# A SwiGLU block: x chunk 0 in two transposing DMAs, eight depth-0 matmuls first, weights in need order over two issuing engines

## The chip, the cores and the metric

One core of one Trainium2 chip. The time is that of one execution on the device, in microseconds (us), without a profile; runs differ by a few tenths of a microsecond, so a difference of less than one per cent needs several rounds on the same chip. A profile is one further look at the same program; its span is about 1.8 us shorter than the time of the same execution.

## The reference

```python
B, S, D, F = 1, 2048, 512, 1376          # bf16 inputs
def reference(x, w_gate, w_up, w_down):
    g = silu(x @ w_gate)
    u = x @ w_up
    return (g * u) @ w_down
```

## The kernel before

Tokens are cut into four chunks of 512, D into four depths of 128, F into ten tiles of 128 and a rest of 96. x is transposed by the DMA on its way in, so that a depth lies on the partitions. For each chunk and tile, TensorE (PE) runs four matmuls for gate and four for up (one per depth, 128x512 each), ScalarE (ACT) applies silu, VectorE (DVE) multiplies. Then 16 token groups are multiplied with w_down. All loads are issued by SyncE (SP), weights in slabs of tiles with all depths:

```python
N_WARM = 11
slabs = [(0, 1), (1, 2), (2, 4), (4, 7), (7, NFT)]
...
def xT_dma(eng, c):
    return eng.dma_start_transpose(
        xT_sb[:, :, c * SC:(c + 1) * SC], xf[c * SC:(c + 1) * SC, :]).then_inc(s_xT[c], 16)

@block.sync
def _(sp):
    xT_dma(sp, 0)
    for si in range(len(slabs)):
        wg_slab_dma(sp, si)
        wu_slab_dma(sp, si)
    ...                                        # rest of up, x chunks 1 to 3, w_down, stores

@block.tensor
def _(pe):
    for i in range(N_WARM):                    # warm-up matmuls on constants
        pe.matmul(banks[7][:, :], lhsT=ones_w, rhs=ones_m, start=True, stop=True)
    for c in range(NSC):
        pe.wait_ge(s_xT[c], 16)
        for ft in range(NFF):
            ...                                # wait for the gate slab and a free bank
            for dk in range(KD): ...           # four gate matmuls into psG[n % 3]
            ...                                # wait for the up slab and a free bank
            for dk in range(KD): ...           # four up matmuls into psU[n % 2]

@block.scalar
def _(act):
    act.activation(adummy[:, 0:4], zero_c, ACT.Silu)   # loads the table early
    ...
```

## Time and profile before

The median was 122.76 us in three runs.

The page of the kernel before: busy time and its share of the span by engine, then the chain that ended last, by engine.

```profile
PE 117.9 (97%) x550; PEld 53.3 (44%) x550; DVE 43.8 (36%) x64; ACT 30.2 (25%) x51; POOL 0.2 (0%) x4
...
PE 97%; DVE 0%; issue 0%
```

PE is the bottleneck. Its head, in the timeline of PE alone (start, duration, engine, line, what, how many, and in brackets how long PE was idle before and what ended that):

```profile
0.77 4.85 PE L167 MATMUL bank<-const-bfloat16-1.0 128*128 128x512 bf16 x11 [0.77 <-PEq L322]
5.54 1.42 PE L179 MATMUL bank<-xT_sb,w_sb 128*128 128x512 bf16 x4
6.79 1.03 PE L191 MATMUL bank<-xT_sb,w_sb 128*128 128x512 bf16 x4
7.66 1.03 PE L179 MATMUL bank<-xT_sb,w_sb 128*128 128x512 bf16 x4
```

The first real matmul starts at 5.54 us. From 6.58 us on they start 0.216 us apart; the warm-up matmuls and the first three real ones start 0.38 to 0.43 us apart, that is at about half speed. The granted clock in the records is 1.00 in all this time, so half speed is read from the starts.

The loads at the head as SP issues them (start and duration of the issue):

```profile
0.74 1.40 SPq L128 DMA_TRANSPOSE xT_sb<-in_x_dram  x1
2.20 0.66 SPq L116 DMA_DIRECT2D w_sb<-in_w_gate_dram  x1
2.92 0.48 SPq L123 DMA_DIRECT2D w_sb<-in_w_up_dram  x1
```

By the trace's semaphore updates, x lands at 4.92 us and the first gate slab (128 KB) at 5.41. The first real matmul needs both; the warm-up matmuls fill the time until then (the last starts at 4.99), so PE is hardly idle.

### The profile page before, as it was taken

What the parts mean: (1) busy time and instruction counts of PE and PEld (TensorE: products, weight loads), DVE (VectorE), ACT (ScalarE), POOL (GpSimd) and SP (SyncE); (2) the same over time, 40 slices, a digit from 0 to 9 for tenths busy, and PEclk for the clock granted to TensorE, in tenths of its full rate; (3) what the DMA queues carried; (4) which work ended last, traced back from release to release, by engine and by line L of the source; (5) the groups of instructions that cost most, each with busy time, mean ns of one, the idle gap of its engine ahead of it and who ended that gap; (6) DMA issues with size and microseconds to landing.
All of it is one profiled execution on the core that took longest, in us unless ns stands there. A gap on an engine that the chain in (4) does not pass through costs nothing.

```text
span 121.1 us, 1391 instructions
## 1 busy us (share of the span) xinstructions
PE 117.9 (97%) x550; PEld 53.3 (44%) x550; DVE 43.8 (36%) x64; ACT 30.2 (25%) x51; POOL 0.2 (0%) x4
## 2 busy tenths in 40 slices
PE   7999999999999999999999999999999999999991
PEld 2244444444444444444444444444444444444470
DVE  0024334444334444334444334467242233224221
ACT  4032333262333272333262333230000000000010
POOL 0000000000000000000000000000000000000000
PEclk9999999999999999999999999999999999999999
DMA  3999999900000000000000000000211211121121
GB/s 67 255 283 372 262 241 225 369 20 0 0 0 0 0 0 5 0 0 3 3 0 0 0 0 0 5 0 0 87 43 43 87 43 49 49 81 43 43 74 56
DMA packets 17990, 8.51 MB, mean 70 GB/s; under 512 B 11360, under 2 KB 17984, under 8 KB 17984
## 3 DMA queue, kind: packets, MB, share of 16 engines
q1 hardware_dynamic: 17984, 8.42, 25.6%
q8 instruction: 4, 0.07, 0.2%
q14 instruction: 2, 0.02, 0.0%
HBM read 4.23 MB, written 2.10 MB: 52 GB/s over the span
## 4 chain that ended last, share of the span: by engine, by line
PE 97%; DVE 0%; issue 0%
PE bank L245 32%; PE bank L179 29%; PE bank L191 29%; PE bank L167 4%; PE bank L204 3%; PE bank L215 2%; DVE o_sb L308 0%; PE bank L220 0%
## 5 line engine op out<-in xcount | busy, mean ns | idle before, releaser
L284 DVE TENSOR_TENSOR hT_sb<-sg_sb,bank 128x512 bf16<-128x512 f32 x40 | 27.5, 688 | 44.9 <-PE bank L191 44.8
L179 PE MATMUL bank<-xT_sb,w_sb 128*128 128x512 bf16 x160 | 41.5, 382 | 0.0
L191 PE MATMUL bank<-xT_sb,w_sb 128*128 128x512 bf16 x160 | 41.1, 379 | 0.0
L245 PE MATMUL bank<-wd_sb,hT_sb 128*128 128x512 bf16 (+3 forms) x187 | 38.3, 367 | 0.0
L261 ACT ACTIVATE sg_sb<-bank 128x512 f32<-128x512 f32 x40 | 23.8, 596 | 44.7 <-PE bank L179 44.7
L245 PEld LDWEIGHTS bank<-wd_sb,hT_sb 128*128 128x128 bf16 (+1 forms) x187 | 18.1, 97 | 20.3 <-issue 0.4
L179 PEld LDWEIGHTS bank<-xT_sb,w_sb 128*128 128x128 bf16 x160 | 15.6, 98 | 19.8 <-DMA xT_sb<-in_x_dram 0.8
L191 PEld LDWEIGHTS bank<-xT_sb,w_sb 128*128 128x128 bf16 x160 | 15.6, 98 | 18.9
L308 DVE CAST o_sb<-bank 128x512 bf16<-128x512 f32 (+1 forms) x16 | 10.8, 675 | 24.9 <-PE bank L245 24.9
L275 ACT ACTIVATE o_sb<-bank 128x256 bf16<-128x256 f32 x1 | 0.4, 383 | 37.6 <-PE bank L245 37.6
L167 PE MATMUL bank<-const-bfloat16-1.0 128*128 128x512 bf16 x11 | 4.9, 628 | 0.8 <-PEq L322 0.8
L289 DVE TENSOR_TENSOR hT_sb<-sgx_sb,bank 32x512 bf16<-32x512 f32 x4 | 2.8, 692 | 5.3 <-ACT sgy_sb L266 5.3
L204 PE MATMUL bank<-xT_sb,w_sb 128*128 128x512 bf16 x16 | 4.1, 379 | 0.0
L265 ACT ACTIVATE sgx_sb<-bank 32x512 f32<-32x512 f32 x4 | 2.4, 588 | 4.5 <-PE bank L204 4.5
L167 PEld LDWEIGHTS bank<-const-bfloat16-1.0 128*128 128x128 bf16 x11 | 1.5, 140 | 3.3 <-issue 3.3
L296 DVE TENSOR_TENSOR hT_sb<-sgy_sb,bank 64x512 bf16<-64x512 f32 x4 | 2.7, 684 | 0.1
L204 PEld LDWEIGHTS bank<-xT_sb,w_sb 128*128 128x128 bf16 x16 | 1.6, 98 | 1.9
L266 ACT ACTIVATE sgy_sb<-bank 64x512 f32<-64x512 f32 x4 | 2.4, 589 | 0.0
L215 PE MATMUL bank<-xT_sb,w_sb 128*64 128x512 bf16 x8 | 1.9, 382 | 0.0
L220 PE MATMUL bank<-xT_sb,w_sb 128*64 128x512 bf16 x8 | 1.9, 382 | 0.0
L254 ACT ACT_TABLE_LOAD x1 | 1.3, 1283 | 0.7 <-PEq L322 0.7
L215 PEld LDWEIGHTS bank<-xT_sb,w_sb 128*64 128x64 bf16 x8 | 0.8, 110 | 1.0 <-issue 0.4
(6 smaller groups left out, 1.4 us busy)
## 6 DMA issues: line engine op xcount, KB each, us to landing
out_dram<-o_sb SPq DMA_DIRECT2D x15, 128.0 KB, 1.7
wd_sb<-in_w_down_dram SPq DMA_DIRECT2D x1, 1280.0 KB, 6.3
w_sb<-in_w_gate_dram SPq DMA_DIRECT2D x1, 480.0 KB, 6.2
w_sb<-in_w_up_dram SPq DMA_DIRECT2D x1, 448.0 KB, 6.8
w_sb<-in_w_gate_dram SPq DMA_DIRECT2D x1, 384.0 KB, 4.8
w_sb<-in_w_up_dram SPq DMA_DIRECT2D x1, 384.0 KB, 5.4
w_sb<-in_w_gate_dram SPq DMA_DIRECT2D x2, 128.0 KB, 3.1
w_sb<-in_w_up_dram SPq DMA_DIRECT2D x2, 128.0 KB, 3.0
```

The source lines that it names most:

```text
L167: pe.matmul(banks[7][:, :], lhsT=ones_w, rhs=ones_m, start=True, stop=True)
L179: ins = pe.matmul(psG[n % NG][:, :], lhsT=w_sb[:, dk, ft * P:(ft + 1) * P], rhs=xT_sb[:, dk, c * SC:(c + 1) * SC], start=(dk == 0), stop=( ...
L191: ins = pe.matmul(psU[n % NU][:, :], lhsT=w_sb[:, dk, UPH + ft * P:UPH + (ft + 1) * P], rhs=xT_sb[:, dk, c * SC:(c + 1) * SC], start=(dk = ...
L204: ins = pe.matmul(psX[:, :], lhsT=w_sb[:, dk, XC0:XC0 + P], rhs=xT_sb[:, dk, c * SC:(c + 1) * SC], start=(dk == 0), stop=(dk == KD - 1),)
L215: pe.matmul(psY[pi][0:64, :], lhsT=w_sb[:, dk, YC0:YC0 + 64], rhs=xT_sb[:, dk, a * SC:(a + 1) * SC], start=(dk == 0), stop=(dk == KD - 1), ...
L245: ins = pe.matmul(psO[bb][:, 0:ncol], lhsT=hT_sb[0:K, fk, t * P:(t + 1) * P], rhs=wd_sb[0:K, fk, c0:c0 + ncol], start=(fk == 0), stop=(fk ...
L261: act.activation(sg_sb[n % NSG][:, :], psG[n % NG][:, :], ACT.Silu).then_inc(s_Gf, 1)
L265: act.activation(sgx_sb[c][96:128, :], psX[64:96, :], ACT.Silu)
L284: dve.tensor_tensor(hT_sb[:, ft, c * SC:(c + 1) * SC], sg_sb[n % NSG][:, :], psU[n % NU][:, :], ALU.mult,).then_inc(s_Uf, 1)
L289: dve.tensor_tensor(hT_sb[64:96, NFF, c * SC:(c + 1) * SC], sgx_sb[c][96:128, :], psX[96:128, :], ALU.mult,).then_inc(s_Xd, 1)
L296: dve.tensor_tensor(hT_sb[0:64, NFF, c * SC:(c + 1) * SC], sgy_sb[c][y0:y1, :], psY[pi][y0:y1, :], ALU.mult,).then_inc(s_Yd, 1)
L308: dve.tensor_copy(o_sb[ob][:, c0:c0 + ncol], psO[bb][:, 0:ncol]).then_inc(s_Of, 1)
```

## The change

The intent is to start real work earlier. Depth 0 of x (128 features) comes in its own transposing DMA, the other 384 in a second. With depth 0 of x and of the first four tiles' weights, PE can start eight accumulations (four gate, four up), one in each of the eight PSUM banks, while the rest is on its way. ACT issues the first weights beside SP. Warm-up matmuls go from 11 to 7. Semaphores become one per engine and one per DMA; the order of the middle and the tail stays.

```diff
-N_WARM = 11
+N_WARM = 7
 ...
-            xT_dma(sp, 0)
-            for si in range(len(slabs)):
-                wg_slab_dma(sp, si)
-                wu_slab_dma(sp, si)
+        HF = 4
+        CUT = 1
+        for k0, k1 in ((0, CUT), (CUT, KD)):
+            o = load_x("sp", 0, k0, k1)
+            ...
+        load_first("act", w_gate, 0, got_g, 0, HF, 0, CUT)          # tiles 0..4, depth 0
+        ready = op("act", lambda e: e.activation(adummy[:, 0:4], zero_c, ACT.Silu))
+        load_first("act", w_up, UPH, got_u, 0, HF, 0, CUT, [ready])
+        load_first("act", w_gate, 0, got_g, 0, 2, CUT, KD)          # tiles 0..2, depths 1..3
+        load_first("sp", w_up, UPH, got_u, 0, 2, CUT, KD)
+        load_first("sp", w_gate, 0, got_g, 2, 4, CUT, KD)
+        load_first("sp", w_up, UPH, got_u, 2, 4, CUT, KD)
+        for a, b in ((4, 7), (7, NFT)): ...                         # slabs of all depths, SP
 ...
+            if c == 0:
+                for mm in (mm_g, mm_u):
+                    for ft in range(HF):
+                        for dk in range(CUT):
+                            mm(ft, 0, ft, dk)
+                for ft in range(HF):
+                    for dk in range(CUT, KD):
+                        g = mm_g(ft, 0, ft, dk)
+                    for dk in range(CUT, KD):
+                        u = mm_u(ft, 0, ft, dk)
+                    evac(ft, 0, ft, g, u)
```

(The rest of the diff rewrites the same instructions in another form.) Below, "deep" means depths 1 to 3, and the "deep gate weights" are those of tiles 0 and 1, 192 KB.

## The prediction

> **What bounds the kernel now.** TensorE: the page gives PE 117.9 of 121.1 us (97%), and so does the chain of waits. In the timeline real matmuls run unbroken from 5.54 to 118.7 us, 0.216 us from start to start (128x512); DVE (36%) and ACT (25%) keep up. Outside lie only the head (11 warm-up matmuls, 0.427 us each) and a tail of 2.4 us (a copy, a store). The change keeps every real matmul, so only the head and a few half-speed matmuls can give time.
>
> **The head before.** The transposing DMA of x chunk 0 (512 KB) is issued at 0.74 us (issue takes 1.40) and lands at 4.92; the first gate slab, issued behind it at 2.20, lands at 5.41; the first matmul starts at 5.54. The first three real matmuls are still 0.38 to 0.43 us apart; full speed comes at about 6.4 us. By 6.8 us four are done. This agrees with the Trainium skill, "TensorE: Matmul & The Clock Gate", Part 1: half rate until a window of about 3.4 us, running free of the kernel's start, was busy.
>
> **What the change moves.**
> - x comes as 128 features, then 384. The whole x took some 2.0 to 4.3 us in packets plus 0.6 to landing. Estimated, the first part has 0.45 us of packets (0.8 shared with the first gate weights, which ACT issues meanwhile) and lands at 3.1 to 3.5 us; the rest at 4.8 to 5.2.
> - Seven warm-up matmuls end at 0.77 + 7x0.427 = 3.8 us. There eight depth-0 matmuls start (four gate, four up, eight banks).
> - The depth-0 up weights are issued on ACT after its table load (1.28 us) and dummy activation, at about 3 us, so they land at 5.2 to 5.6, as four half-speed gate matmuls (3.8 to 5.5) end. The depth-1-to-3 gate weights, third on ACT, land at 6.2 to 6.8.
> - So all eight are done by about 6.8 us, against four before: 4 x 0.216 = 0.86 us gained. Then PE should run unbroken: tiles 0 to 3 take 6 matmuls (1.3 us) each, above ACT's 0.60 and DVE's 0.69; the slab of tiles 4 to 6, which landed at 10.49 and 11.58 before, is issued sooner and needed at about 12.
> - Two issuing engines share the DMA engines (the Trainium skill, "DMA: Bandwidth & Descriptors", section "Issuing engines are not separate DMA queues"): the gain is issue time and order, not bandwidth.
> - Middle and tail: same instructions and waits, nothing gained.
>
> All of it is on the critical path, TensorE's. The most is the eight matmuls, 1.73 us; stalls of 0 to 0.5 us for depth-1-to-3 weights can eat part.
>
> **Prediction.** 122.76 - 0.9 = 121.9 us, range 121.3 to 122.5. Faster by over 2% (below 120.3) 3%, within 2% 95%, slower 2%.
>
> **What would show it.** First real matmul at 3.7 to 4.0 us; eight done by 6.5 to 7.1; x's first part landed before 3.6, its second before 5.2; PE idle under 0.5 us before the first up or depth-1 matmul; everything after 7 us earlier by 0.7 to 1.1 us at unchanged 0.216 us spacing; span about 120.2.
>
> **What would make it wrong.** A narrow transposing DMA with nearly the full one's latency (after 4.5 us: no gain); the 384 features or the depth-1-to-3 weights after 7 us (gain near zero); PE idle in the head, so that full speed comes a window later (a loss of about 1 us); full speed much earlier than 6.4 us, so that data alone decide; a late slab of tiles 4 to 6.

## More of the kernel before

DMA traffic in windows (window, length, busy times of PE, PEld, VectorE, ScalarE and GpSimd, granted clock, DMA share, GB/s; the share adds up packet times and can exceed 1):

```profile
2.50:3.00 0.50, 0.50 (x3) 0.22 (x2) 0.00 (x0) 0.00 (x0) 0.00 (x0) 1.00 1.18 246
3.00:3.50 0.50, 0.50 (x3) 0.16 (x2) 0.00 (x0) 0.00 (x0) 0.00 (x0) 1.00 1.27 289
3.50:4.00 0.50, 0.50 (x2) 0.15 (x1) 0.00 (x0) 0.00 (x0) 0.00 (x0) 1.00 1.27 288
```

Once packets flow, they flow without a gap, at 246 to 289 GB/s in these windows.

## The result and the profile after

The kernel after took 122.80 us (median of four runs, 122.75 to 123.25) against 122.68 for the kernel before in the same rounds: ratio 1.0013, 95% interval 0.9989 to 1.0036. A ratio here is the mean time of one kernel's fast runs over that of the other's in the same rounds, so not quite the ratio of the medians quoted. A second job of five rounds gave 1.0032 (1.0014 to 1.0051), 123.02 against 122.59. The forecast 0.9 us is not there; if anything the kernel became 0.1 to 0.4 us slower.

The page of the kernel after, the same lines: DMA and ACT now stand in the chain.

```profile
PE 116.9 (97%) x546; PEld 52.7 (44%) x546; DVE 43.8 (36%) x64; ACT 30.2 (25%) x51; POOL 0.2 (0%) x4
...
PE 92%; DMA 4%; ACT 1%; ACTq 1%; DVE 0%; issue 0%
```

PE's head in the timeline:

```profile
0.77 3.14 PE L176 MATMUL bank<-const-bfloat16-1.0 128*128 128x512 bf16 x7 [0.77 <-PEq L331]
3.71 1.91 PE L179 MATMUL bank<-xT_sb,w_sb 128*128 128x512 bf16 x4
6.01 1.04 PE L179 MATMUL bank<-xT_sb,w_sb 128*128 128x512 bf16 x4 [0.39 <-DMA w_sb<-in_w_up_dram]
7.46 1.89 PE L179 MATMUL bank<-xT_sb,w_sb 128*128 128x512 bf16 x8 [0.41 <-DMA w_sb<-in_w_gate_dram]
```

Real work starts at 3.71 us as forecast, and then waits twice. The brackets understate the waits, because a matmul's modelled end overlaps the next start. From start to start the fifth matmul came 1.02 us after the fourth, 0.59 more than the half-speed spacing of 0.43; the ninth came 0.79 after the eighth, 0.58 more than 0.216. So the lead over the kernel before melts:

| start of real matmul | before | after | lead |
|---|---|---|---|
| 1st | 5.54 | 3.71 | 1.83 |
| 5th | 6.79 | 6.01 | 0.78 |
| 9th | 7.66 | 7.46 | 0.20 |
| 17th | 9.38 | 9.18 | 0.20 |
| last | 118.38 | 118.18 | 0.20 |

Part of this is no loss: four matmuls at half speed are worth only 0.86 us of full speed. But of the 0.86 us that I expected to keep, only 0.20 was left at the ninth, and about 0.1 more went in the tail of this profile. In the second job's profile the ninth matmul came at 7.79, later than before's 7.66. The chain of waits says what the ninth waited for (start, length, what):

```profile
2.67 0.35 ACTq L128
3.03 0.03 issue
3.06 4.27 DMA w_sb<-in_w_gate_dram
7.33 0.14 issue
7.46 1.67 PE bank L179 x7
```

The deep gate weights, issued by ACT at 3.06, were 4.27 us on their way. The packet records divide this (on ACT's queue these weights alone have packets of 512 bytes): 2.46 us until the first packet at 5.52, behind the up weights; 1.45 us until the last packet ended at 6.97, while 193 KB passed on SP's queue; 0.36 us to the landing. The issues of SP and ACT at the head:

```profile
0.74 1.22 SPq L123 DMA_TRANSPOSE xT_sb<-in_x_dram  x1
2.02 1.46 SPq L124 DMA_TRANSPOSE xT_sb<-in_x_dram  x1
3.53 0.58 SPq L130 DMA_DIRECT2D w_sb<-in_w_up_dram  x1
```

```profile
0.73 0.38 ACTq L128 DMA_DIRECT2D w_sb<-in_w_gate_dram  x1
1.14 1.28 ACT L151 ACT_TABLE_LOAD   x1 [1.14 <-PEq L331]
2.44 0.20 ACT L151 ACTIVATE act_dummy<-const-float32-0.0 128x4 f32<-128x4 f32 x1
2.67 0.35 ACTq L128 DMA_DIRECT2D w_sb<-in_w_up_dram  x1
3.06 0.46 ACTq L130 DMA_DIRECT2D w_sb<-in_w_gate_dram  x1
```

The issue of a quarter of x took 1.22 us, where the whole of x took 1.40. Only then could the second part be issued. The same windows as before show the hole that this leaves:

```profile
2.50:3.00 0.50, 0.50 (x3) 0.22 (x2) 0.00 (x0) 0.14 (x1) 0.00 (x0) 1.00 0.76 165
3.00:3.50 0.50, 0.50 (x3) 0.03 (x2) 0.00 (x0) 0.00 (x0) 0.00 (x0) 1.00 0.10 24
3.50:4.00 0.50, 0.50 (x2) 0.23 (x2) 0.00 (x0) 0.00 (x0) 0.00 (x0) 1.00 0.94 220
```

From 3.0 to 3.5 us 24 GB/s moved, where the kernel before moved 289. Where each transfer landed, by the semaphore updates of one profile per kernel (us; forecast in the first row), and when the ninth real matmul started:

| kernel | x, first part | x complete | depth-0 gate | depth-0 up | deep gate | 9th matmul |
|---|---|---|---|---|---|---|
| forecast | 3.1 to 3.5 | 4.8 to 5.2 | - | 5.2 to 5.6 | 6.2 to 6.8 | 6.8 |
| before | - | 4.92 | 5.41 (slab) | 5.86 (slab) | - | 7.66 |
| after | 3.44 | 6.38 | 2.95 | 5.96 | 7.33 | 7.46 |
| after_again | 3.46 | 6.32 | 2.98 | 5.88 | 7.66 | 7.79 |
| split_only | 3.42 | 5.66 | 6.58 (slab) | 7.12 (slab) | - | 8.44 |
| x_whole | - | 4.82 | 2.88 | 6.46 | 7.78 | 8.25 |
| x_whole_w11 | - | 5.00 | 3.00 | 6.77 | 8.07 | 8.12 |
| up_early | 4.69 | 6.66 | 3.18 | 4.44 | 6.53 | 6.70 |
| up_early_w9 | 4.33 | 5.64 | 3.00 | 4.00 | 7.64 | 7.78 |
| all_early | 4.07 | 6.96 | 2.96 | 3.85 | 5.54 | 7.13 |
| after_w11 | 3.48 | 6.16 | 3.02 | 5.76 | 7.58 | 7.71 |
| no_deep_wait | 3.42 | 6.12 | 2.91 | 5.74 | 7.81 | 6.83 |
| sp_deep | 3.43 | 6.22 | 2.99 | 5.84 | 7.79 | 7.93 |
| sp_all | 3.42 | 6.30 | 2.85 | 4.79 | 7.35 | 7.48 |
| sp_up | 3.44 | 7.59 | 2.87 | 4.54 | 6.06 | 7.64 |
| early_t0_w8 | 4.92 | 6.72 | 3.00 | 3.91 | 5.36 (tile 0) | 7.06 |
| before_act_w10 | - | 5.23 | 3.19 (slab) | 5.67 (slab) | - | 7.13 |

Two profiles of the same kernel (after, after_again) differ by 0.33 us in the deep gate weights, so smaller differences in this table carry no verdict.

### The profile page after: what moved, and what is told of

Same layout as the page of the kernel before. It is cut to its first block, busy times and chain, and to the rows that moved or that the text cites. A ratio compares the mean times of both kernels' runs of the same rounds, so it can differ in the third digit from the quotient of the medians.

```text
span 121.1 us, 1376 instructions
## 1 busy us (share of the span) xinstructions
PE 116.9 (97%) x546; PEld 52.7 (44%) x546; DVE 43.8 (36%) x64; ACT 30.2 (25%) x51; POOL 0.2 (0%) x4
## 4 chain that ended last, share of the span: by engine, by line
PE 92%; DMA 4%; ACT 1%; ACTq 1%; DVE 0%; issue 0%
PE bank L179 59%; PE bank L277 32%; DMA w_sb<-in_w_gate_dram 4%; PE bank L251 2%; ACT L151 1%; ACTq L128 1%; DVE o_sb L285 0%; ACT act_dummy L151 0%
## 5 line engine op out<-in xcount | busy, mean ns | idle before, releaser
L179 PE MATMUL bank<-xT_sb,w_sb 128*128 128x512 bf16 x336 | 73.9, 382 | 0.8 <-DMA w_sb<-in_w_gate_dram 0.4
L176 PE MATMUL bank<-const-bfloat16-1.0 128*128 128x512 bf16 x7 | 3.1, 624 | 0.8 <-PEq L331 0.8
L251 PE MATMUL bank<-xT_sb,w_sb 128*64 128x512 bf16 x16 | 1.9, 382 | 0.0
L176 PEld LDWEIGHTS bank<-const-bfloat16-1.0 128*128 128x128 bf16 x7 | 0.9, 135 | 2.1 <-issue 2.1
```

The costliest lines, as they stand in the source:

```text
L176: op("pe", lambda e: e.matmul(banks[7][:, :], lhsT=ones_w, rhs=ones_m, start=True, stop=True), inc=False)
L179: return op("pe", lambda e: e.matmul(bank[:, :], lhsT=w_sb[:, dk, col0:col0 + P], rhs=xT_sb[:, dk, c * SC:(c + 1) * SC], start=(dk == 0), ...
L251: ym = op("pe", lambda e, pi=pi, dk=dk, c=c, y0=y0, y1=y1: e.matmul(psY[pi][y0:y1, :], lhsT=w_sb[:, dk, YC0:YC0 + 64], rhs=xT_sb[:, dk, c ...
```

## The experiments

My first theory, A: the second transposing DMA costs a whole issue on SP, and ACT's later weights are held up behind it. Rival B: the DMA engines' bandwidth, the same bytes having to come in any order. Rival C: the table load in front of ACT's second issue. All ratios are to the kernel before on the same chip, five rounds, unless said otherwise. All results were correct except the two that are wrong on purpose.

### Is the wait for the deep weights worth the missing gain? (no_deep_wait)

```diff
# matmuls of chunk 0, tiles 0 to 3: depths 1 to 3 read depth 0 again (wrong result on purpose)
+            sk = 0 if c == 0 and ft < HF else dk
-            deps = [got_x[c, dk], got_g[ft, dk]]
+            deps = [got_x[c, sk], got_g[ft, sk]]
```

> Wrong result on purpose: in the kernel after, the matmuls of depth 1 to 3 of the first four tiles read the depth-0 weights and features again, so they wait for no deep weights and not for the second part of x; the loads stay as they are. If the wait for the deep weights (0.57 us in the profile of after) is a loss on the critical path, the ninth matmul starts at 6.85 to 6.95 us instead of 7.46 in a run with full speed at 6.0, and the time falls by 0.4 to 0.6 us: ratio to before 0.995 to 0.998. If the lost time comes from elsewhere (clock, tail), the ratio stays at 1.000 to 1.002.

Measured: ratio 0.9950 (0.9933 to 0.9967), 122.18 us, runs from 122.08 to 122.43. PE's head:

```profile
3.71 1.91 PE L180 MATMUL bank<-xT_sb,w_sb 128*128 128x512 bf16 x4
5.79 3.58 PE L180 MATMUL bank<-xT_sb,w_sb 128*128 128x512 bf16 x15 [0.17 <-DMA w_sb<-in_w_up_dram]
```

The loads are the same (deep gate weights at 7.81), but the second wait is gone; the ninth matmul starts at 6.83, 0.83 us ahead of the kernel before, and 0.83 us is also the lead at the last matmul. That is close to the 0.86 us of the prediction; in the times without a profile the gain is 0.6 us. So the arithmetic of the critical path was right, and one thing is missing: the data in time. The run removes the waits for the second part of x and for all deep weights of the first four tiles together; that the deep gate weights are the ones that ended the wait is read from the landings of the kernel after (7.33, against 6.38 for x). The wait for the up weights remains here and does not stop this gain.

### What does the split cost by itself? (split_only)

```diff
# in the kernel before
-            xT_dma(sp, 0)
+            for a, b in ((0, 1), (1, KD)):
+                dst = xT_sb[:, 0, 0:SC] if b == 1 else xT_sb[:, a:b, 0:SC]
+                sp.dma_start_transpose(dst, xf[0:SC, a * P:b * P]).then_inc(s_xT[0], 16)
-                pe.wait_ge(s_xT[c], 16)
+                pe.wait_ge(s_xT[c], 32 if c == 0 else 16)
```

> The kernel before with x chunk 0 in transposing DMAs of 128 and 384 features, nothing else. If the second transposing DMA costs a whole issue plus start (its issue began at 2.02 us and its first packet came at 3.3 in the kernel after), x is complete at 5.6 to 6.0 us even with no other traffic, instead of 4.92, the gate slab lands at 6.1 to 6.5 instead of 5.41, and the time rises by 0.4 to 0.8 us: ratio 1.003 to 1.007. If the second part was late only because other weights were in the way, x is complete by 5.2 us and the ratio is 0.999 to 1.002.

Measured: ratio 1.0127 (1.0079 to 1.0174), more than expected. x was complete at 5.66 instead of 4.92, with no other load issued before or between its two parts, and the gate slab behind it landed at 6.58 instead of 5.41. The traffic of its windows has the same hole:

```profile
2.50:3.00 0.50, 0.50 (x3) 0.23 (x2) 0.00 (x0) 0.00 (x0) 0.00 (x0) 1.00 0.44 93
3.00:3.50 0.50, 0.50 (x3) 0.16 (x2) 0.00 (x0) 0.00 (x0) 0.00 (x0) 1.00 0.09 22
3.50:4.00 0.50, 0.50 (x2) 0.15 (x1) 0.00 (x0) 0.00 (x0) 0.00 (x0) 1.00 0.93 211
```

So 0.74 us of the second part's lateness is the price of the second transposing DMA alone (one profile of each kernel; x issued whole landed at 4.82 to 5.23 in five profiles), and what is issued behind it pays 1.17 us; in the kernel after (6.38 and 6.32) another 0.7 us comes on top, with the traffic of ACT's weights in between. In this profile PE then stood idle for 1.79 us; its matmuls were at full speed afterwards, but runs up to 125.5 us suggest (not shown) that this idle stretch sometimes costs clock as well, of which more below.

### Undoing the split, weights in need order kept (x_whole, x_whole_w11)

```diff
-        for k0, k1 in ((0, CUT), (CUT, KD)):
+        for k0, k1 in ((0, KD),):
```

> Undoes only the split of x chunk 0; the weights stay in need order on two engines and the eight depth-0 matmuls stay first. Theory A (the second transposing DMA costs a whole issue of about 1.2 us on SyncE, and ACT's later weights are held up behind it): x lands at 4.9 us as in the kernel before, the depth-0 up weights by 5.1 and the depth-1-to-3 gate weights by 6.4, so the eight are done by about 6.9 us without an idle wait over 0.2 us, and PE runs 0.5 to 0.7 us ahead of the kernel after, ratio to before 0.993 to 0.996. Theory B (the DMA engines' bandwidth is what delays the weights, since the same bytes must come): the depth-1-to-3 gate weights still land at 7.2 to 7.4, and the time stays that of the kernel after, ratio about 1.001.

Measured: ratio 1.0095 (1.0060 to 1.0129). A miss for both theories. x landed at 4.82 as expected, but PE's matmuls went on at half speed:

```profile
0.77 3.15 PE L176 MATMUL bank<-const-bfloat16-1.0 128*128 128x512 bf16 x7 [0.77 <-PEq L331]
4.86 7.40 PE L179 MATMUL bank<-xT_sb,w_sb 128*128 128x512 bf16 x23 [0.95 <-DMA xT_sb<-in_x_dram]
```

After an idle 0.95 us the starts were 0.427 us apart until 9.51 us, then 0.216. The deep gate weights landed at 7.78, not earlier than in the kernel after, which speaks against A as the whole cause. It is no clean test, though: without the second transposing DMA SP issued the deep up weights at 2.20 instead of 3.53, and they landed at 6.18, ahead of weights that are needed first; 1685 KB had moved when the deep gate weights landed. No run has x whole with the deep gate weights issued ahead of all that is needed later. To see what the idle stretch did, the same with 11 warm-up matmuls:

```diff
-N_WARM = 7
+N_WARM = 11
```

> x chunk 0 whole as in the run x_whole, but with 11 warm-up matmuls, so PE has no idle stretch from 3.7 to 4.9 us. If x_whole lost its 1.2 us because the idle stretch put off full speed (its matmuls stayed 0.427 us apart until 9.5 us), full speed comes at 6.2 to 6.6 us here, the ninth matmul starts at about 7.7 to 7.9 (deep gate weights landed at 7.78 there), ratio to before 0.999 to 1.003, runs within 0.5 us. If it lost it to weights that land later, the ratio stays at 1.008 to 1.010.

Measured: ratio 1.0037 (1.0016 to 1.0058), full speed already at 4.0 us in the profile, ninth matmul at 8.12. So about 0.6% of the 0.95% goes with the idle stretch, and the rest with the late weights (deep gate at 8.07). An idle stretch need not cost this: in the profile of up_early, below, PE idled 0.83 us before its first real matmul (from 3.91 to 4.74) and ran at full speed from it on. The varying moment of full speed agrees with the Trainium skill, "TensorE: Matmul & The Clock Gate", Part 1, which says that the array runs at half rate until a window of about 3.4 us was busy and that the window runs free of the kernel's start: with PE busy without a gap from 0.77 us on, full speed came at 4.0 us here and at about 6.4 in the kernel before; with the idle stretch of x_whole at 9.5.

### Fewer warm-ups in the kernel before (before_w7)

```diff
# in the kernel before
-N_WARM = 11
+N_WARM = 7
```

> The kernel before with 7 warm-up matmuls, nothing else: PE idles from about 3.8 to 5.5 us. If an idle stretch in the head puts off full speed, matmuls stay 0.427 us apart until somewhere between 7 and 9.5 us in the profiled run: a loss of 0.3 to 1.5 us that differs from run to run (spread over 0.7 us), ratio 1.004 to 1.012. If not, ratio 0.999 to 1.001.

Measured: three runs at 122.53 to 122.65 us and four at 124.47 to 124.66, which count as slow and are left out of the ratio, 0.9981 (0.9956 to 1.0006). By the fast runs the warm-up count makes no difference. The run settles nothing about the idle stretch, because a run counts as slow when it is over 1.5% above the fastest, whatever the reason, and so a run that lost that much to the clock would be left out too.

### The early start (after_w11)

```diff
-N_WARM = 7
+N_WARM = 11
```

> The kernel after with the 11 warm-up matmuls of the kernel before, so that its real matmuls start at 5.5 us instead of 3.7. If the weights and the second part of x are what it waits for (they land at 6.0 to 7.4 us however early PE starts), the early start is worth nothing: the ninth real matmul (the first that needs the second part of x) still starts at 7.3 to 7.6 us, and the time is that of the kernel after, ratio to before 0.999 to 1.003, with runs closer together because PE no longer idles while its clock rises. If the early start does pay, it loses the four half-speed matmuls, 0.86 us: ratio 1.006 to 1.009.

Measured: ratio 1.0018 (0.9999 to 1.0037), the same as the kernel after within the intervals, although real work began at 5.33 instead of 3.71:

```profile
5.33 1.89 PE L179 MATMUL bank<-xT_sb,w_sb 128*128 128x512 bf16 x8
7.71 1.46 PE L179 MATMUL bank<-xT_sb,w_sb 128*128 128x512 bf16 x6 [0.49 <-DMA w_sb<-in_w_gate_dram]
```

Eight matmuls fit between 5.33 and 7.1, and then PE waits for the same DMA (landed at 7.58). The head of the kernel after is set by its data; starting 1.6 us earlier buys nothing.

### ACT's weights before the table load (up_early, up_early_w9, all_early)

```diff
# up_early; up_early_w9 also has N_WARM = 9
         load_first("act", w_gate, 0, got_g, 0, HF, 0, CUT)
+        load_first("act", w_up, UPH, got_u, 0, HF, 0, CUT)
         ready = op("act", lambda e: e.activation(adummy[:, 0:4], zero_c, ACT.Silu))
-        load_first("act", w_up, UPH, got_u, 0, HF, 0, CUT, [ready])
-        load_first("act", w_gate, 0, got_g, 0, 2, CUT, KD)
+        load_first("act", w_gate, 0, got_g, 0, 2, CUT, KD, [ready])
```

> Depth-0 up weights issued by ACT before its table load instead of after. Theory A: they land at 3.3 to 3.6 us instead of 5.96, the first part of x at 3.5 to 3.9, the idle wait of 0.6 us before the up matmuls is gone, but the depth-1-to-3 gate weights still land at 7.0 to 7.4, so the wait only moves there (1.0 to 1.2 us in one piece) and the time changes by under 0.3 us: ratio 0.998 to 1.001. Theory C (the table load in front of the up weights is the whole loss): the time falls by the 0.6 us of that wait, ratio 0.995 to 0.997.

Measured: ratio 1.0020 (0.9987 to 1.0053), runs from 122.09 to 123.60. The up weights landed at 4.44 and the first wait was gone, but the first part of x slipped from 3.44 to 4.69. The profiled run was the fastest of the six (ninth matmul at 6.70). Theory C's forecast (0.995 to 0.997) missed: taking the table load out of the way didn't lower the time. What the table load costs by itself is not isolated, because 128 KB now went ahead of x.

> The run up_early with 9 warm-up matmuls instead of 7, which fill the idle stretch from 3.7 to 4.7 us that PE had there. If its runs from 122.09 to 123.6 us differ by when full speed comes and the idle stretch is to blame, they now lie within 0.6 us and the ratio falls from 1.002 to 0.995 to 0.999. If the spread comes from the DMAs, it stays over 1 us and the ratio at 1.000 to 1.003.

Measured: ratio 1.0006 (0.9982 to 1.0029), runs from 122.59 to 123.31. The spread shrank from 1.5 to 0.7 us, the gain did not come: with x complete already at 5.64, the deep gate weights landed at 7.64.

```diff
# all_early: all three before the table load
         load_first("act", w_gate, 0, got_g, 0, HF, 0, CUT)
-        ready = op(...)
-        load_first("act", w_up, UPH, got_u, 0, HF, 0, CUT, [ready])
+        load_first("act", w_up, UPH, got_u, 0, HF, 0, CUT)
         load_first("act", w_gate, 0, got_g, 0, 2, CUT, KD)
+        op("act", lambda e: e.activation(adummy[:, 0:4], zero_c, ACT.Silu))
```

> All three weight DMAs of ACT (depth-0 gate, depth-0 up, depth-1-to-3 gate of tiles 0 and 1) issued before the table load, so before the second part of x is issued. Theory A: gate, up and deep gate weights land at about 3.0, 3.5 and 4.6 us, the first part of x by 4.4, its second part at 6.2 to 6.5, both idle waits shrink to under 0.3 us in sum, eight matmuls done by 6.9 us, 0.5 to 0.6 us ahead of the kernel after: ratio to before 0.993 to 0.997. Theory B: the bytes are the same, so what is brought forward pushes x back as much: second part of x at 6.8 to 7.3 us and the time that of the kernel after, ratio about 1.000.

Measured: ratio 0.9983 (0.9963 to 1.0003), runs from 122.36 to 122.76. The deep gate weights landed at 5.54, but now the second part of x came at 6.96, as B has it for the landing; the time lies between the two theories.

### The second part of x as a plain DMA (xb_plain, one look, wrong result on purpose)

```diff
-            o = load_x("sp", 0, CUT, KD)
+        o = dma("sp", lambda e: e.dma_start(
+            xT_sb[:, 1:KD, 0:SC], w_down[0:3 * P, :].rearrange("(k p) d -> p k d", p=P)))
```

> Wrong result on purpose: the second part of x is replaced by a plain DMA of as many bytes (384 KB) from the down weights; all else is the kernel after. Theory A: SyncE's issue of it takes about 0.5 us instead of 1.46, ACT's depth-0 up weights, still issued at 2.67 us, have their first packet at about 3.6 us (0.97 us after issue, as ACT's first DMA) instead of 4.5 and land before 5.1; the deep gate weights land before 6.3. Theory B (bandwidth): the up weights still land after 5.6 us.

Measured: SP's issue took 0.56 us, as A said, but ACT's depth-0 up weights still landed at 6.24 and the deep gate weights at 7.54; the time of its one run was 123.06 us. So the lateness of ACT's weights does not need a second transposing DMA beside it, and A's forecast for the weights (before 5.1 and 6.3) missed; what stays of A is the price for x itself (split_only). Not clean: SP also issued the deep up weights earlier, at 2.64 instead of 3.53, so they competed more.

### More work per first part (cut2, cut2_up_w9)

If PE starves after eight matmuls, a cut after depth 2 gives it sixteen.

```diff
-        CUT = 1
+        CUT = 2
```

> One number of the kernel after changed: x and the first weights are cut after depth 2 instead of depth 1, so sixteen matmuls, not eight, need nothing but the first part of x. x's first part (256 KB) lands at 4.0 to 4.5 us, so PE idles 0.3 to 0.8 us after its 7 warm-up matmuls; from then on it has work until the second part (6.4 to 6.9 us) and the deep weights (under 8.2 us) are in, without waits over 0.3 us. If full speed comes by 6.4 us: the 17th matmul at 8.6 to 8.9 us against 9.38 before, ratio 0.993 to 0.997. If the idle stretch puts off full speed to 7 to 9.5 us: ratio 1.000 to 1.008, runs over 0.7 us apart.

Measured: ratio 1.0113 (1.0081 to 1.0145). The first part of x, 256 KB beside 256 KB of depth-0-and-1 gate weights, landed at 5.59, not 4.0 to 4.5; it was complete at 9.18. With up_early's order and nine warm-up matmuls:

> The cut after depth 2 with the first up weights issued by ACT before its table load and 9 warm-up matmuls, which end at 4.6 us when the first part of x (expected at 4.4 to 5.0) comes in: no idle stretch, so full speed at 4.4 to 6.6 us, sixteen matmuls without waits over 0.3 us, the 17th at 8.1 to 9.0 us against 9.38. Ratio 0.991 to 0.997 and runs within 0.6 us, if data and idle stretches were the causes; about 1.000 if bringing up weights forward delays x by as much as it gains.

Measured: ratio 1.0080 (1.0036 to 1.0124) by four fast runs, two of six slow; the first part of x landed at 6.57 (in a profile of a slow run). Both fail: a first part that is bigger, with more weights beside it, comes later than the whole of x came before.

### The same bytes in one queue (sp_deep, sp_all, sp_up, after_again)

My next theory: two queues take turns on the DMA engines, so the deep gate weights on ACT share with the deep up weights on SP, which are needed later.

```diff
# sp_deep
-        load_first("act", w_gate, 0, got_g, 0, 2, CUT, KD)
+        load_first("sp", w_gate, 0, got_g, 0, 2, CUT, KD)
```

> One word of the kernel after changed: the depth-1-to-3 gate weights of tiles 0 and 1 are issued on SyncE's queue, between the second part of x and the depth-1-to-3 up weights, instead of third on ACT's. Sharing theory (two queues take turns on the DMA engines, so the deep gate weights, needed first, run at half rate beside the deep up weights and land with them): in one queue they land at 6.6 to 6.9 us instead of 7.33, the wait before the ninth matmul shrinks from 0.57 to under 0.15 us, the ninth starts at 6.85 to 7.05, ratio to before 0.995 to 0.998. Bytes theory (they are late because x and the depth-0 weights come first, whatever the queue): they land after 7.1, ratio 0.999 to 1.002.

Measured: ratio 1.0027 (1.0008 to 1.0046); deep gate weights at 7.79.

```diff
# sp_all: SP issues x part 1, depth-0 up, x part 2, deep gate, deep up ...; ACT only depth-0 gate
+        first_x(0, CUT)
         load_first("act", w_gate, 0, got_g, 0, HF, 0, CUT)
-        load_first("act", w_up, UPH, got_u, 0, HF, 0, CUT, [ready])
-        load_first("act", w_gate, 0, got_g, 0, 2, CUT, KD)
+        load_first("sp", w_up, UPH, got_u, 0, HF, 0, CUT)
+        first_x(CUT, KD)
+        load_first("sp", w_gate, 0, got_g, 0, 2, CUT, KD)
```

> As sp_deep, and the depth-0 up weights go on SyncE's queue too, between the two parts of x (ACT issues only the depth-0 gate weights). Sharing theory: the up weights fill the stretch from 3.0 to 3.5 us in which the DMA engines stood nearly idle and land at 3.9 to 4.5, the second part of x lands at 5.7 to 6.2, deep gate at 6.3 to 6.7, deep up at 6.9 to 7.3; PE has no idle wait over 0.1 us from 0.77 us on and the ninth matmul starts at 6.2 to 7.0: ratio 0.991 to 0.996, runs within 0.5 us. Bytes theory: the same bytes in front, so the deep gate weights still land after 7.1 us and the ratio is 0.999 to 1.002.

Measured: ratio 1.0040 (1.0016 to 1.0063). PE's head:

```profile
3.71 3.08 PE L181 MATMUL bank<-xT_sb,w_sb 128*128 128x512 bf16 x8
7.48 1.89 PE L181 MATMUL bank<-xT_sb,w_sb 128*128 128x512 bf16 x8 [0.70 <-DMA w_sb<-in_w_gate_dram]
```

The first wait is gone (up weights at 4.79); the second has taken it over. The deep gate weights landed at 7.35, although nothing was in front of them in their queue that was needed later.

> As sp_all but with the deep gate weights left on ACT (behind its table load): tells which of the two moves does it. Sharing theory: up weights at 3.9 to 4.5 us, but deep gate weights and second part of x slow each other, one of them lands at 6.4 to 7.0; ninth matmul at 6.4 to 7.1, ratio 0.992 to 0.997. Bytes theory: 0.999 to 1.002.

(sp_all with the deep gate weights on ACT, behind its table load.) Measured: ratio 1.0021 (1.0001 to 1.0041); deep gate weights at 6.06, x complete at 7.59.

> The kernel after unchanged, for its ratio and spread on the same chip as these three: 0.999 to 1.003, ninth matmul at 7.3 to 7.8 us, deep gate weights landed 0.1 us earlier.

Measured: 1.0032 (1.0014 to 1.0051), deep gate weights at 7.66, ninth matmul at 7.79. None of the three differs from it by more than the intervals. The sharing theory falls as the whole cause: whichever order and queue, the last of x and deep gate weights landed at 7.35 to 7.79 in these four.

### Fewer bytes ahead (early_t0_w8, before_act_w10)

```diff
# early_t0_w8: all_early, but on ACT only the deep gate weights of tile 0, the rest tile by tile on SP
-N_WARM = 7
+N_WARM = 8
+        load_first("act", w_gate, 0, got_g, 0, 1, CUT, KD)
+        op("act", ...)                                      # table load after ACT's three issues
+        load_first("sp", w_up, UPH, got_u, 0, 1, CUT, KD)
+        load_first("sp", w_gate, 0, got_g, 1, 2, CUT, KD)
+        load_first("sp", w_up, UPH, got_u, 1, 2, CUT, KD)
```

> As all_early (ratio 0.998), but the deep gate weights brought forward on ACT are those of tile 0 alone (96 KB instead of 192), the others follow on SyncE tile by tile, and 8 warm-up matmuls fill the 0.4 us that PE idled there. Fewer bytes ahead: the second part of x, which ended the head of all_early at 6.96 us, lands at 6.3 to 6.8, the ninth matmul starts at 6.5 to 7.0, ratio 0.993 to 0.997. If slow packets at the start of each stream, not bytes, set these times: second part of x still at 6.8 to 7.3, ratio 0.998 to 1.001.

Measured: ratio 0.9935 (0.9916 to 0.9954) by four fast runs, 121.86 to 122.42 us; two of six runs, 124.01 and 124.55, are left out (with them the mean is 122.86, that of the kernel before 122.83, so the gain holds for the fast runs only). x complete at 6.72, ninth matmul at 7.06, and PE without a wait from its first real matmul on:

```profile
0.77 3.57 PE L178 MATMUL bank<-const-bfloat16-1.0 128*128 128x512 bf16 x8 [0.77 <-PEq L333]
4.96 4.20 PE L181 MATMUL bank<-xT_sb,w_sb 128*128 128x512 bf16 x17 [0.62 <-DMA xT_sb<-in_x_dram]
```

```diff
# before_act_w10: the kernel before; N_WARM = 10; its first gate slab is issued by ACT
+            wg_slab_dma(act, 0)
             act.activation(adummy[:, 0:4], zero_c, ACT.Silu)
```

> The kernel before with one part of the change alone, a second issuing engine: its first gate slab (128 KB) is issued by ACT at 0.73 us instead of second on SyncE at 2.20; 10 warm-up matmuls. Bytes theory: the slab lands at 3.0 and x, pushed back by it, at 5.0 to 5.3 (640 KB are needed for the first matmul in both kernels, so the start moves little, from 5.54 to 5.1 to 5.4): ratio 0.997 to 1.000. If the order of issue had been the bottleneck, the start would be that of x alone, 5.0 us, with full speed unchanged, and the ratio 0.995 to 0.997.

Measured: ratio 0.9969 (0.9951 to 0.9988), 122.38 us, all six runs fast, 122.19 to 122.93. The gate slab landed at 3.19, x at 5.23, pushed back by it, and the first matmul came at 5.28, then no wait:

```profile
5.28 1.16 PE L180 MATMUL bank<-xT_sb,w_sb 128*128 128x512 bf16 x4
6.27 1.03 PE L192 MATMUL bank<-xT_sb,w_sb 128*128 128x512 bf16 x4
7.13 1.03 PE L180 MATMUL bank<-xT_sb,w_sb 128*128 128x512 bf16 x4
```

Its ninth matmul, at 7.13, is earlier than that of the whole change, 7.46 and 7.79. Both of these versions beat both kernels in their fast runs. Of the two I would keep before_act_w10: its gain is smaller, but none of its runs fell into the slower group.

## Why the prediction was wrong

- **"What bounds the kernel now": right.** no_deep_wait, which removes the second wait in the head, moves the last matmul by as much as the ninth, 0.83 us.
- **"x comes as 128 features, then 384 ... lands at 3.1 to 3.5 us": right for the first part** (3.44). **"The rest at 4.8 to 5.2": wrong, and the first step that failed.** It came at 6.38 and 6.32. I had scaled packets with size and taken the issue as hidden. The trace has 1.22 us for the issue of a quarter against 1.40 for the whole, then a hole of half a microsecond in the traffic. split_only puts 0.74 us on that alone; the other 0.7 us comes with ACT's weights between. At 6.38 it did not itself stop PE, which was busy with the eight until about 6.9; it took time on the DMA engines from what came behind it. Moving one of the two transposing DMAs to ACT, to have both in flight, is no way out: the Trainium skill, "DMA: Bandwidth & Descriptors", section "DMA Transpose (X-bar)", warns that two transposing streams in flight at once can silently corrupt each other; no run here tries it.
- **"Seven warm-up matmuls end at ... 3.8 us. There eight depth-0 matmuls start": right** (3.71).
- **"The depth-0 up weights ... land at 5.2 to 5.6": late**, at 5.96, a wait of 0.59 us. It was not the costly one: in sp_all this wait is gone and the ratio is 1.0040, in up_early it is gone and the ratio is 1.0020.
- **"The depth-1-to-3 gate weights, third on ACT, land at 6.2 to 6.8": wrong, and this is the step that took the gain.** They landed at 7.33 and 7.66. Their first packet went at 5.52, behind the late up weights, and they shared the DMA engines with SP's loads. no_deep_wait gives the value of that wait, with that for x removed too: ratio 0.9950 against about 1.002.
- **"So all eight are done by about 6.8 us, against four before": done by about 6.9 in the profile of the kernel after, but the next matmul had to wait until 7.46**, where the kernel before had done eight as well by 7.66. The forecast listed "the depth-1-to-3 weights after 7 us (gain near zero)" among what would make it wrong; that is what happened.
- **"PE idle in the head, so that full speed comes a window later": not seen in the profile of the kernel after** (its fifth to eighth matmuls are at full speed), but seen in that of x_whole, where half speed lasted until 9.51 us after an idle 0.95 us; x_whole_w11, without the idle stretch, lost 0.6% less.
- **"Two issuing engines share the DMA engines ... the gain is issue time and order, not bandwidth": agrees with the runs:** from 2.0 to 7.5 us the kernel before moved 245 GB/s on average and the kernel after 238. I quoted it and didn't follow it. The kernel before needs x (512 KB) and 128 KB of weights to run on, 640 KB; the kernel after needs x, 256 KB of depth-0 weights and 192 KB of deep gate weights before its ninth matmul, 960 KB. An estimate from the traces: the kernel before brought its 640 KB in 3.3 us, from its first packet at 2.1 us to the landing at 5.41; at that pace 960 KB from the first packet at 1.7 us take 4.95 us, to 6.6 us. With the half microsecond of hole that makes 7.1. Measured were 7.33 and 7.66. Two things qualify this sum. For its own ninth matmul the kernel before needs 896 KB (x and three slabs), which had landed by 6.34 us, while PE was busy: the sum at the ninth matmul hardly changed, the time at which PE asks for it did. And loads that are needed later pass with those needed now: by the packet records 1255 KB had moved when the deep gate weights landed in the kernel after (1370 in after_again), where 960 were needed, and 796 when the first slab landed in the kernel before, where 640 were. Counting all of it, as an estimate, 1255 KB at the 248 GB/s of the kernel before take 5.2 us, to 6.9, with the hole 7.4.

Why the time is slightly worse while the profile of the kernel after leads by 0.20 us: the profiled run of the kernel before has a span of 121.15 us, while its other runs lie at 120.5 to 121.3. An estimate, not shown: a kernel that is limited by PE gains when full speed happens to come early, one that waits for data at 7.3 to 7.8 us does not.

**What stays open.** That the deep weights are late, and what that costs, is shown. Why they never landed before 7.3 us in the orders of sp_deep, sp_all and after is not settled. The needed bytes alone give the 6.6 us of the estimate above. The later loads that pass beside them fit the kernel after, but not sp_all: there 1123 KB had moved at 7.35, at only 207 GB/s from its first packet on. The packet records of several runs hold single packets of 0.3 to 1.4 us, where 0.02 to 0.05 us is usual, often near the start of a stream; whether order, addresses or neighbours cause them was not tried. early_t0_w8 changed three things against all_early's parent order (bytes ahead, tile by tile, one more warm-up) and so supports the bytes reading without proving it. Why two of its runs were slow is open too.

## What to carry to other kernels

Before splitting a load to start earlier, add up the bytes that must land before the engine can run *without stopping again*, not before it can start; if the split raises that sum (640 to 960 KB here), the early start is spent waiting. Count the later loads that will be in flight beside them too. Charge a further transposing DMA for its own issue and start (here 0.74 us for x and 1.17 us for what was issued behind it, for a cut into 128 and 384 features; no other cut was timed alone). An early start at half speed is worth half, and an idle microsecond in the head can put off full speed, so judge such a change by the start of the first matmul after which there is no more wait, and by several unprofiled runs.

## What the Trainium skill lacked or had wrong

- "DMA: Bandwidth & Descriptors", section "DMA Transpose (X-bar)", has no issue time or fixed cost by size of a transposing DMA, and the rest of the page gives bandwidths and cycle counts of other transposes. Here the issue took 1.22 us for 128 features of 512 tokens, 1.46 for 384 and 1.40 for 512, and splitting one into two made x complete 0.74 us later with no other load issued before it (split_only).
- The same page, section "Issuing engines are not separate DMA queues": the runs agree that no bandwidth is gained (245 GB/s before, 238 after, from 2.0 to 7.5 us). What it lacks is how late a second engine's DMA can start; the page has one first-byte latency for DMAs issued by SP or ACT, about 0.6 us, and does not tell a first DMA from a second. In the packet records ACT's first DMA had its first packet 1.01 us after the start of its issue (0.73 to 1.74), its second 1.84 us after (2.67 to 4.51), and about as late, 1.87 us, with a plain DMA instead of the transposing one on SP (xb_plain). The 0.97 us in that run's expectation was read from a coarser view.
- "TensorE: Matmul & The Clock Gate", Part 1, agrees in that full speed came at varying times, from 4.0 to 9.5 us in the profiles of fast runs here. It speaks of idle gaps of over 3.4 us. What it lacks is what a shorter gap does before full speed is reached: in x_whole the matmuls stayed 0.427 us apart until 9.51 us after an idle 0.95 us, with the granted clock recorded as 1.00 throughout, while in up_early full speed followed an idle 0.83 us at once.
